# Dealing the opening order of a fused attention and SwiGLU kernel anew, with its squares summed on TensorE and constant filler products from the first instruction

## The chip, the cores and the metric

The kernel runs on one core of one Trainium2 chip. The metric is device time in microseconds (us), as the median of several runs. PE is TensorE's matmul side and PEld its weight loads, DVE is VectorE, ACT is ScalarE, POOL is GpSimd, SP is SyncE (it issues DMAs). All arithmetic is float32.

## The reference

Two stages. The first is a cross attention between 512 tokens and 32 states in each of 8 batches and 8 heads; the second is a SwiGLU feed-forward network over all 8 x (512 + 32) = 4352 rows of 512.

```python
def _attn_ref(x, state):                     # x: 8,8,512,64   state: 8,8,32,64
    scores = x @ state.T / sqrt(64)          # per batch and head
    a = softmax(scores);      xread = a @ state
    scores2 = state @ x.T / sqrt(64)
    a2 = softmax(scores2);    sread = a2 @ x
    return concatenate([xread, sread], axis=2)

def _moe_ref(x, w_gate, w_val, w_out, rms_g):   # x: 4352,512
    xn = x / sqrt(mean(x * x) + 1e-6) * rms_g
    g, val = xn @ w_gate, xn @ w_val            # 512 -> 1536
    return (silu(g) * val) @ w_out              # 1536 -> 512
```

The three weight matrices arrive as float64; `x` and `state` arrive as float32.

## The kernel before, in words

**Algebra.** A token's attention read is a product of its 256 softmax weights (8 heads x 32 states) with the states. The kernel therefore folds the states of a batch into the weights once: `own_weights(b, mp)` multiplies the states (times `rms_g`, tile `stT_g`, L390) with a block `w_m` of `w_gate` and `w_val` (L528) and copies the result to `v` (L539). The hidden layer of the batch is then `v` times the transposed softmax weights `aT_s`. The scale of the RMS norm is multiplied into `aT_s` (L434), so nothing of the hidden layer can start before that instruction.

**Tokens of a batch** (`tokens_read(b)`): transposes of `x_b` on TensorE (L298 for the first two batches) with copies (L300), scores (L307), a 32 x 32 transpose on VectorE (L316), softmax (L378 to L403), the reads (L410), their squares on ScalarE (L417, four tiles `sq`), three additions of the squares on VectorE (L420), a sum over partitions by four products with a column of ones (L424), the power -1/2 on GpSimd (L270), a spread of it by transposes (L277), and L434.

**States of a batch** (`states_read(b)`): maxima (L446), exponentials (L452), transposes (L459) and copies (L461), products with `x_b` (L471), scaling (L478), a transpose (L482) and a copy (L484). After L471 the tile `x_b` of the batch is free; there are two of them, so the loads of batch 2's `x` (16 DMAs, L122) wait for L471 of batch 0, and those of batch 3 for L471 of batch 1.

**Weights.** The float64 weights are loaded in 18 pieces of 1 MB (`load_piece`, L186), four pieces ahead. Each piece is turned to float32 by three ScalarE steps (`exponents()`, L215, L217, L220) and four VectorE steps (`values()`, L241, L244, L248, L253); the first piece goes in two halves. Six converted pairs `w_m` are stored to DRAM (`w_d`, L257) and loaded again for every batch (`fetch`, L168) into three buffers.

**Batch 0** uses plain products: hidden layer at L570, Silu at L576, gate at L580, output projection at L776. From batch 1 on both layers use a seven-product scheme (L674 hidden, L836 projection), with sums of the weights' blocks prepared on VectorE (`weight_sums`, L817) and on GpSimd (`more_of_v`, `slot_sums`, L592 to L595).

**The order.** TensorE, VectorE and ScalarE execute what `tc.manual_schedule` records, in that order. Each piece of work is a generator, and a string of letters says which generator makes its next step. `ORDER` covers batch 0 and the preparation of batch 1: `a` and `s` are tokens and states of batch 0, `A` and `S` those of batch 1, `e` and `d` the conversion, `v` the weights of batch 0, `h`, `t`, `u` its hidden layer, `p` and `c` its projection, `w` the first weights of batch 1, `k` the sums of `wo`, and `z` one filler product whose result nobody reads (`keep_awake`, L927). `PERIOD` orders each of the batches 1 to 7, and `STATES` the last stage over the 256 state rows. SP's queue follows the order in which the steps issue DMAs.

When the first `c` or `k` is met, the pools of the conversion are closed and the later ones opened:

```python
            if stream in "ck" and "s" not in seven:
                early.close()
                open_late()
                slot_sums(1)
```

Of the kernel before, what the change touches and what calls it, by code (L numbers as in the profile page):

```python
# [8 lines left out]
F32 = mybir.dt.float32  # L9
# [8 lines left out]
P = 128  # L18
# [1 line left out]
W_BUFS = 3  # L20

ORDER = (
    "aaaaaaaaddaaaaaaeaseeaasadsasszzzzzzzzzzzzzzssdsaaaasaeadesaeeazzsdasaaezzzzzzza"
    "deadaaaddeeazzzzsedaadszzzzzadaeedzzvvavdzzadeaAzzzzhdeeddtdAdAAhueheAeedtddphAe"
    "dvdvduvdphedeAedtdhApeehddeuAdddeAhdedvdtudvvpeAAAAdhdAAteAehuhpddephepdeAdAeApA"
    "dteedAAvvveAdpudAAephtdSdhAdphdeAueedhAdeAteudddeeSppAddAAdppAdAdevApvdveehhAdth"
    "AudhpdeddeedeAdteAupvdvdvphedAAtdShhutSAhpukSSSkkkwSwkpSkpwpSSckSScckkpcSwkkkwww"
    "w"
)

PERIOD = (
# [12 lines left out]
def kernel(  # L44
# [21 lines left out]
    VE, SE, GE, TE = nc.vector, nc.scalar, nc.gpsimd, nc.tensor  # L66
# [5 lines left out]
    NC = S // P  # L72
# [18 lines left out]
    seven = {}  # L91

    early = ExitStack()
# [23 lines left out]
    def load_x(b, *queues):  # L117
# [8 lines left out]
        for c in range(NC):  # L126
            (queues or (nc.sync,))[c % max(1, len(queues))].dma_start(
                out=x_sb[b][:, c].rearrange("p (h d) -> p h d", h=H),
                in_=x[b, :, P * c:P * c + P, :].rearrange("h p d -> p h d"))

    ident = consts.tile([P, P], F32, name="ident")
    make_identity(nc, ident)
    mhalf = consts.tile([P, NC], F32, name="mhalf")
    GE.memset(mhalf, -0.5)
    ones = consts.tile([P, 1], F32, name="ones")
# [131 lines left out]
    def mean_root(ss, n):  # L267

        ri = two.tile([P, NC], F32, name="ri")
        GE.tensor_tensor(out=ri[:, 0:n], in0=ss, in1=mhalf[:, 0:n], op=ALU.pow)  # L270
        return ri

    def along_rows(ri, n):

        rp = aps.tile([P, NC, P], F32, name="at")
        for c in range(n):
            TE.transpose(out=rp[:, c, :], in_=ri[:, c:c + 1].to_broadcast([P, P]), identity=ident)  # L277
        return rp.rearrange("p c t -> p (c t)")
# [88 lines left out]
    def tokens_read(b):  # L367
        packed, soft = rows.pop(b), {}
        yield from (scores if b < 2 else scores_of_blocks)(b, packed, soft)
        half = soft["half"]  # L370
        m1 = two.tile([P, 2, S // Ns], F32, name="m1")
        z1 = two.tile([P, 2, S // Ns], F32, name="z1")

        def along(t, e):
            return t[:, e].unsqueeze(2).to_broadcast([P, S // Ns, Ns])

        for e in range(2):
            VE.reduce_max(out=m1[:, e], in_=half(e), axis=AXX)  # L378
            yield
            VE.tensor_tensor(out=half(e), in0=half(e), in1=along(m1, e), op=ALU.subtract)  # L380
            yield
            SE.activation(out=half(e), in_=half(e), func=ACTF.Exp, scale=SCALE)
            yield "step"
        stT_g[b] = two.tile([P, 4, Ns], F32, name="stT_g")
        if b > 1:
            soft["st"] = aps.tile([P, 4, Ns], F32, name="at")
            TE.transpose(out=soft["st"].rearrange("p j n -> p (j n)"),
                         in_=packed.rearrange("p e d -> p (e d)"), identity=ident)
            yield
        VE.tensor_tensor(out=stT_g[b], in0=soft["st"], in1=rms_g.unsqueeze(2).to_broadcast([P, 4, Ns]),  # L390
                         op=ALU.mult)
        yield
        aT_s[b] = two.tile([P, 2, S], F32, name="aT_s")
        for e in range(2):
            VE.reduce_sum(out=z1[:, e], in_=half(e), axis=AXX)
            yield
            VE.tensor_scalar(z1[:, e], z1[:, e], 1e-9, None, op0=ALU.add)
            VE.reciprocal(z1[:, e], z1[:, e])
            yield
            VE.tensor_tensor(out=half(e), in0=half(e), in1=along(z1, e), op=ALU.mult)  # L400
            yield
            for to, blocks in soft["back"](e):
                VE.transpose(out=to, in_=blocks)  # L403
            yield "step"


        reads = [(aps, vps)[j // 2].tile([P, S], F32, name=("at", "pv")[j // 2]) for j in range(4)]
        for j in range(4):
            for e in range(2):
                TE.matmul(out=reads[j][D * e:D * e + D, :],  # L410
                          lhsT=packed[Ns * j:Ns * j + Ns, e, :],
                          rhs=aT_s[b][Ns * j:Ns * j + Ns, e],
                          start=True, stop=True)
        yield
        sq = one.tile([P, 4, S], F32, name="sq", tag="xT")
        for i, j in enumerate((2, 3, 0, 1)):
            SE.activation(out=sq[:, i, :], in_=reads[j], func=ACTF.Square, scale=DM ** -0.5)  # L417
            yield "step" if i == 3 else None
        for i, j in ((0, 1), (2, 3), (0, 2)):
            VE.tensor_tensor(out=sq[:, i, :], in0=sq[:, i, :], in1=sq[:, j, :], op=ALU.add)  # L420
            yield
        sp = aps.tile([P, NC], F32, name="at")
        for c in range(NC):
            TE.matmul(out=sp[:, c:c + 1], lhsT=sq[:, 0, P * c:P * c + P], rhs=ones,  # L424
                      start=True, stop=True)
        yield
        ss = two.tile([P, NC], F32, name="ss")
        VE.tensor_scalar(ss, sp, 1e-6, None, op0=ALU.add)
        yield "step"
        ri = mean_root(ss, NC)  # L430
        yield
        rp = along_rows(ri, NC)
        yield
        VE.tensor_tensor(out=aT_s[b], in0=aT_s[b],  # L434
                         in1=rp.unsqueeze(1).to_broadcast([P, 2, S]), op=ALU.mult)
        yield "step"
# [79 lines left out]
    def own_weights(b, mp):  # L516


        pv = []

        def products():
            w = w_sb.pop(b * (NM // 2) + mp)
            for e in range(2):
                pv.append(vps.tile([P, 4 * P], F32, name="pv") if b and mp % 2 == 0 else
                          aps.tile([P, 4 * P], F32, name="at"))
            for j in range(4):
                for e in range(2):
                    TE.matmul(out=pv[e][Ns * j:Ns * j + Ns, :],  # L528
                              lhsT=stT_g[b][D * e:D * e + D, j, :],
                              rhs=w[D * e:D * e + D, j].rearrange("p m k f -> p (m k f)"),  # L530
                              start=True, stop=True)
            fetch(b * (NM // 2) + mp + W_BUFS)
            yield

        def copies():
            v = (seven["v"] if b else v_0).tile([P, 2, 2, 2, P], F32, name="v")
            v_sb[b, mp] = v, None
            for e in range(2):
                SE.copy(v[:, e].rearrange("p m k f -> p (m k f)"), pv[e])  # L539
                yield  # L540
            if b:
                more_of_v(b, mp)
                yield

        return products(), copies()
# [42 lines left out]
    def slot_sums(b):  # L588

        tt = aT_t[b] = seven["late"].tile([P, 3, HS], F32, name="aT_t")  # L590
        b11, b12, b21, b22 = (aT_s[b][:, e, HS * i:HS * i + HS] for e in range(2) for i in range(2))
        GE.tensor_tensor(out=tt[:, 0], in0=b12, in1=b11, op=ALU.subtract)  # L592
        GE.tensor_tensor(out=tt[:, 1], in0=b22, in1=tt[:, 0], op=ALU.subtract)
        GE.tensor_tensor(out=tt[:, 2], in0=b21, in1=tt[:, 1], op=ALU.subtract)
        GE.tensor_tensor(out=b12, in0=b22, in1=b12, op=ALU.subtract)  # L595
# [304 lines left out]
    def store_tokens(b):  # L900
        def store(r, c0, n, ot):
            r0 = T * b + P * r
            nc.sync.dma_start(out=out[r0:r0 + P, c0:c0 + n], in_=ot)
        return store
# [17 lines left out]
    def keep_awake():  # L922


        ps = fz.tile([P, 2, P], F32, name="f")
        while True:
            TE.matmul(out=ps, lhsT=ident, rhs=ident.unsqueeze(1).to_broadcast([P, 2, P]),  # L927
                      start=True, stop=True)
            yield

    def first_of_batch(b):
        for mp in range(2):
            for part in own_weights(b, mp):
                yield from part
# [32 lines left out]
                            mybir.EngineType.Activation})  # L967
    with tc.manual_schedule(**by_hand):
        for stream in ORDER:
            if stream in "ck" and "s" not in seven:  # L970
                early.close()
                open_late()
                slot_sums(1)
            next(streams[stream])
    assert all(next(stream, done) is done for name, stream in streams.items() if name != "z")
    load_state(2)
# [2 lines left out]
    for b in range(1, B):  # L979
# [6 lines left out]
        p, c, k = project_seven(S, store_tokens(b))  # L986
# [6 lines left out]
        if b + 1 < B:  # L993
            streams.update(a=tokens_read(b + 1), s=states_read(b + 1),
                           w=first_products(b + 1, then))
# [9 lines left out]
    n = B * (NM // 2)  # L1005
    h, t, u = hidden_seven(NT, (state_weights, state_sums), state_tokens, True,
                           lambda mp: fetch(n + mp + W_BUFS))
    p, c, k = project_seven(NT, store_states, nc.scalar)
# [34 lines left out]
```

## Time and profile before

| | us |
|---|---|
| median of 5 runs | 791.89 (790.74 to 792.19) |
| the profiled execution | 792.19 |
| its span, first to last instruction | 790.0 |

| engine | busy us | share of the span |
|---|---|---|
| PE | 777.8 | 98% |
| PEld | 604.1 | 76% |
| DVE | 521.4 | 66% |
| ACT | 334.2 | 42% |
| POOL | 171.0 | 22% |

The share of an engine is an average over stages with different limits. From 15 to 110 us VectorE is busy for more than 9.6 of every 10 us, later for about 6.6 of every 10. The chain of waits is the list of what ended last, followed back from the last instruction; an entry gives its start, its length and the work. In a timeline an entry gives the start, the length, the engine, line, operation and operands, how many instructions were merged, and in square brackets the idle time before it and what ended it. One float32 product appears as two records on PE; a transpose appears as one.

### The profile page before, as it was taken

The page shows a single profiled execution, that of the slowest core. Times are in us where ns is not written, and L with a number is a line of the kernel's source. Part 1 is how long each engine was busy: PE and PEld are TensorE (multiplying, and loading weights), DVE is VectorE, ACT ScalarE, POOL GpSimd, SP SyncE. Part 2 cuts the span into 40 slices and gives each one's busy share as a digit, 9 for nine tenths or more (in the row PEclk, how much of TensorE's full clock was granted, in tenths as well). Part 3 has the DMA queues.
Part 4 walks back from the last instruction along what each step waited for, and adds up shares of the span by engine and source line. Part 5 has one row for each costly group of instructions (what it writes and reads, how often), then busy time and mean ns, then how long its engine had stood idle before and what let it go on. Part 6 is the DMA issues. An engine that isn't in the chain of part 4 may idle for free.

```text
span 790.0 us, 13559 instructions
## 1 busy us (share of the span) xinstructions
PE 777.8 (98%) x5478; PEld 604.1 (76%) x5478; DVE 521.4 (66%) x822; ACT 334.2 (42%) x560; POOL 171.0 (22%) x216
## 2 busy tenths in 40 slices
PE   6999999999999999999999999999999999999998
PEld 4643444788878887888878887888788887888996
DVE  4999997688338951887268833895188725781461
ACT  4998874552245323542255124532353225410320
POOL 0100003430244023420433024402341043400000
PEclk9999999999999999999999999999999999999999
DMA  9788865730075005610263007500530024201311
GB/s 286 211 288 311 275 189 168 217 122 1 24 223 197 2 17 176 218 35 17 92 215 121 1 24 216 205 2 14 197 153 12 13 93 162 107 5 36 121 54 27
DMA packets 69277, 95.77 MB, mean 121 GB/s; under 512 B 46432, under 2 KB 54112, under 8 KB 62304
## 3 DMA queue, kind: packets, MB, share of 16 engines
q1 hardware_dynamic: 67040, 94.33, 36.4%
q8 instruction: 43, 0.70, 0.4%
q10 hardware_dynamic: 2176, 0.59, 0.3%
q14 instruction: 18, 0.15, 0.1%
HBM read 79.69 MB, written 15.20 MB: 120 GB/s over the span
## 4 chain that ended last, share of the span: by engine, by line
PE 94%; DVE 5%; DMA 0%; issue 0%; ACT 0%; SPq 0%
PE f L674 37%; PE f L836 35%; PE f L776 5%; PE pv L570 4%; PE at L528 3%; PE pv L528 3%; PE at L471 1%; DVE ex L248 1%; PE at L410 1%; PE at L346 1%; PE at L459 1%; PE at L424 1%; DVE raw L244 1%; PE pv L346 1%; PE at L298 1%; DMA rows<-in_state_dram 0%
## 5 line engine op out<-in xcount | busy, mean ns | idle before, releaser
L836 PE MATMUL f<-wo,hb 128*128 128x256 f32 x540 | 123.4, 380 | 0.2 <-ACT ot L873 0.2
L674 PE MATMUL f<-aT_s,v 128*128 128x256 f32 x504 | 120.6, 382 | 0.1
L836 PEld LDWEIGHTS f<-wo,hb 128*128 128x128 f32 x540 | 101.4, 190 | 13.6 <-ACT ot L873 0.4
L674 PEld LDWEIGHTS f<-aT_s,v 128*128 128x128 f32 x504 | 94.1, 190 | 19.6 <-DVE c L736 5.0
L736 DVE TENSOR_TENSOR g<-g,f 128x512 f32<-128x512 f32 (+1 forms) x96 | 61.8, 652 | 68.5 <-PE f L674 64.0
L674 PE MATMUL f<-aT_t,vs 128*128 128x256 f32 x336 | 87.1, 381 | 0.0
L270 POOL TENSOR_TENSOR ri<-ss,mhalf 128x4 f32<-128x4 f32 x8 | 13.5, 1692 | 321.3 <-DVE s L449 210.9
L727 ACT ACTIVATE hb<-g 128x1024 f32<-128x1024 f32 (+1 forms) x48 | 48.2, 1004 | 79.2 <-DVE g L736 79.2
L836 PE MATMUL f<-wt,hs 128*128 128x256 f32 x360 | 81.0, 381 | 0.0
L836 PEld LDWEIGHTS f<-wt,hs 128*128 128x128 f32 x360 | 67.3, 190 | 14.1 <-issue 5.1
L674 PEld LDWEIGHTS f<-aT_t,vs 128*128 128x128 f32 x336 | 63.2, 190 | 15.0 <-issue 5.9
L873 ACT COPY ot<-f 128x256 f32<-128x256 f32 x60 | 21.4, 373 | 123.0 <-PE f L836 123.0
L554 POOL TENSOR_TENSOR vs<-v 128x256 f32<-128x256 f32 x42 | 31.4, 748 | 164.2 <-ACT v L539 164.1
L739 DVE SCALAR_TENSOR_TENSOR hb<-hb,g 128x1024 f32<-128x1024 f32 x42 | 53.2, 1266 | 4.6 <-ACT hb L727 4.6
L725 ACT COPY g<-f 128x512 f32<-128x512 f32 (+1 forms) x48 | 26.9, 561 | 55.8 <-PE f L674 55.8
L776 PE MATMUL f<-wo,hb 128*128 128x512 f32 x96 | 44.7, 600 | 0.0
L557 POOL TENSOR_TENSOR vs<-v,vs 128x256 f32<-128x256 f32 x42 | 44.4, 1057 | 0.0
L570 PE MATMUL pv<-aT_s,v 128*128 128x512 f32 x96 | 43.7, 594 | 0.2 <-DVE aT_s L434 0.2
L674 PE MATMUL f<-aT_t,v 128*128 128x256 f32 x168 | 43.1, 379 | 0.0
L674 PE MATMUL f<-aT_s,vs 128*128 128x256 f32 x168 | 43.1, 379 | 0.0
L836 PE MATMUL f<-wo,hs 128*128 128x256 f32 x180 | 41.1, 379 | 0.0
L836 PEld LDWEIGHTS f<-wt,hb 128*128 128x128 f32 x180 | 33.7, 190 | 9.4 <-DVE ot L881 5.0
(144 smaller groups left out, 1278.3 us busy)
## 6 DMA issues: line engine op xcount, KB each, us to landing
w_m<-w_d SPq DMA_DIRECT2D x48, 1024.0 KB, 6.3
out_dram<-ot SPq DMA_DIRECT2D x56, 128.0 KB, 1.8
raw<-in_moe_w_val_dram SPq DMA_DIRECT2D x6, 1024.0 KB, 5.6
raw<-in_moe_w_out_dram SPq DMA_DIRECT2D x6, 1024.0 KB, 8.6
x_b<-in_x_dram SPq DMA_DIRECT2D x96, 64.0 KB, 2.8
w_d<-w_m SPq DMA_DIRECT2D x6, 1024.0 KB, 4.9
raw<-in_moe_w_gate_dram SPq DMA_DIRECT2D x5, 1024.0 KB, 6.8
x_b<-in_x_dram SPq DMA_DIRECT2D x6, 256.0 KB, 5.9
```

The source lines that it names most:

```text
L528: TE.matmul(out=pv[e][Ns * j:Ns * j + Ns, :], lhsT=stT_g[b][D * e:D * e + D, j, :], rhs=w[D * e:D * e + D, j].rearrange("p m k f -> p (m k ...
L554: GE.tensor_tensor(out=vs[:, 0], in0=a21, in1=a22, op=ALU.add)
L557: GE.tensor_tensor(out=vs[:, 2], in0=a12, in1=vs[:, 1], op=ALU.subtract)
L570: TE.matmul(out=to[0], lhsT=lhs(i, k), rhs=r, start=(i == 0), stop=(i == len(rhs) - 1))
L674: TE.matmul(out=ps[:, i, 0:half], lhsT=l[:, i, :], rhs=r, start=(start and i == 0 and k == 0), stop=(k == len(lhs) - 1), skip_group_check= ...
L725: SE.copy(gates(q)[1], q["x"][:, :, 0:half])
L727: SE.activation(out=hb[:, 2 * mp:2 * mp + 2, 0:n].rearrange("p m (c t) -> p m c t", c=2), in_=q["g"][:, :, :, 0:half], func=ACTF.Silu if s ...
L736: VE.tensor_tensor(out=to, in0=to, in1=q[ps][:, :, 0:half], op=ALU.add)
L739: VE.scalar_tensor_tensor(out=h, in0=h, scalar=1.0, op0=ALU.add, op1=ALU.mult, in1=q["g"].rearrange("p m c t -> p m (c t)"))
L776: TE.matmul(out=banks[r], lhsT=hb[:, m, P * r:P * r + P], rhs=wo[:, m, :], start=(m == 0), stop=(m == NM - 1))
L836: TE.matmul(out=banks[name][:, r, :], lhsT=lhs(k)[:, P * r:P * r + P], rhs=rhs(k), start=(start and r == 0 and k == 0), stop=(k == HM - 1) ...
L873: SE.copy(to, banks[name][:, r, :])
```

## The change

Four things are edited.

1. `ORDER` is dealt anew: the same steps, with 38 fillers instead of 40. Six fillers stand at its head and 20 in a row after the scores of batch 0. The states of batch 0 (`s`), which were done between the scores and the hidden layer, stand near the end of the string, beside those of batch 1.
2. For batch 0 the three additions of squares on VectorE are left out. Instead 16 products with the column of ones, four for each of the four tiles, add up in the same PSUM columns.
3. The filler multiplies a tile `still`, filled with 1.0 by VectorE, with itself, instead of the identity that GpSimd makes.
4. `slot_sums(1)` on GpSimd becomes the first step of `w`, and `w` also closes the early pools.

```diff
@@ -20,12 +20,11 @@
 ORDER = (
-    "aaaaaaaaddaaaaaaeaseeaasadsasszzzzzzzzzzzzzzssdsaaaasaeadesaeeazzsdasaaezzzzzzza"
-    "deadaaaddeeazzzzsedaadszzzzadaeedzzvvavdzzadeaAzzzzhdeeddtdAdAAhueheAeedtddphAe"
...
-    "AudhpdeddeedeAdteAupvdvdvphedAAtdShhutSAhpukSSSkkkwSwkpSkpwpSSckSScckkpcSwkkkwww"
-    "w"
+    "zzzzzzaaaaaaaaadaedeezzaaaaaaaaaaeeaaaaaaeaeaaazzzzzzzzzzzzzzzzzzzzaeaaaeddddadd"
+    "zzzzaadddeedaaadzvdaeevddzzaeavdedzzAzhdAeAdtheeheuhAdddAdpetAeduedevvdpvepAhdAe"
...
+    "ddAdAAvAedAvAdpAsvAhSSetdhuShAdhtukkAASwsSkwkkwSpSSSSkpcpSkwskkkckSwpcSSscskwwww"
 )
@@ -128,6 +127,8 @@
+    still = early.enter_context(tc.tile_pool(name="still", bufs=1)).tile([P, 2, P], F32, name="still")
+    VE.memset(still, 1.0)
     ident = consts.tile([P, P], F32, name="ident")
@@ -416,14 +417,17 @@
-        for i, j in ((0, 1), (2, 3), (0, 2)):
+        for i, j in () if b == 0 else ((0, 1), (2, 3), (0, 2)):
             VE.tensor_tensor(out=sq[:, i, :], in0=sq[:, i, :], in1=sq[:, j, :], op=ALU.add)
             yield
         sp = aps.tile([P, NC], F32, name="at")
-        for c in range(NC):
-            TE.matmul(out=sp[:, c:c + 1], lhsT=sq[:, 0, P * c:P * c + P], rhs=ones,
-                      start=True, stop=True)
-        yield
+        n = 4 if b == 0 else 1
+        for i in range(n):
+            for c in range(NC):
+                TE.matmul(out=sp[:, c:c + 1], lhsT=sq[:, i, P * c:P * c + P], rhs=ones,
+                          start=(i == 0 and c == 0), stop=(i == n - 1), skip_group_check=True)
+            yield
@@ -924,11 +928,13 @@
         ps = fz.tile([P, 2, P], F32, name="f")
         while True:
-            TE.matmul(out=ps, lhsT=ident, rhs=ident.unsqueeze(1).to_broadcast([P, 2, P]),
+            TE.matmul(out=ps, lhsT=still[:, 0], rhs=still,
                       start=True, stop=True)
             yield
 
     def first_of_batch(b):
+        slot_sums(b)
+        yield
         for mp in range(2):
@@ -967,10 +973,9 @@
         for stream in ORDER:
-            if stream in "ck" and "s" not in seven:
+            if stream in "ckw" and "s" not in seven:
                 early.close()
                 open_late()
-                slot_sums(1)
             next(streams[stream])
```

The lines of the changed kernel stand up to five higher: L307 is L308 after the change, L316 is L317, L434 is L438, L570 is L574, L674 is L678.

On SP, 27 loads of `x` in a row (11 of batch 2, 16 of batch 3) now stand between the reloads of the fifth and the sixth `w_m` of batch 1; before, 13 stood there.

More of the change, by code (lines that the diff above doesn't have):

```diff
@@ L22 @@
 ORDER = (
-    "aaaaaaaaddaaaaaaeaseeaasadsasszzzzzzzzzzzzzzssdsaaaasaeadesaeeazzsdasaaezzzzzzza"
-    "deadaaaddeeazzzzsedaadszzzzzadaeedzzvvavdzzadeaAzzzzhdeeddtdAdAAhueheAeedtddphAe"
-    "dvdvduvdphedeAedtdhApeehddeuAdddeAhdedvdtudvvpeAAAAdhdAAteAehuhpddephepdeAdAeApA"
-    "dteedAAvvveAdpudAAephtdSdhAdphdeAueedhAdeAteudddeeSppAddAAdppAdAdevApvdveehhAdth"
-    "AudhpdeddeedeAdteAupvdvdvphedAAtdShhutSAhpukSSSkkkwSwkpSkpwpSSckSScckkpcSwkkkwww"
-    "w"
+    "zzzzzzaaaaaaaaadaedeezzaaaaaaaaaaeeaaaaaaeaeaaazzzzzzzzzzzzzzzzzzzzaeaaaeddddadd"
+    "zzzzaadddeedaaadzvdaeevddzzaeavdedzzAzhdAeAdtheeheuhAdddAdpetAeduedevvdpvepAhdAe"
+    "dtedddehAueheddApdddepvevhdddevdtdupeddeAeehAtshppAAdhduhdedddeeAveeApvdpvdstued"
+    "edAddehhtpddehetpuAddshpvdeuAsedvspAAAAApveshAhAsdtAdudedhedsehtAsAApupdeeAedApp"
+    "ddAdAAvAedAvAdpAsvAhSSetdhuShAdhtukkAASwsSkwkkwSpSSSSkpcpSkwskkkckSwpcSSscskwwww"
 )
```

## The prediction

> **What bounds the kernel now.** I read the page's chain first, because it says which engine to follow.
>
> ```profile
> span 790.0 us, 13559 instructions
> ...
> PE 777.8 (98%) x5478; PEld 604.1 (76%) x5478; DVE 521.4 (66%) x822; ACT 334.2 (42%) x560; POOL 171.0 (22%) x216
> ...
> PE 94%; DVE 5%; DMA 0%; issue 0%; ACT 0%; SPq 0%
> ```
>
> TensorE is the path for 94%. The diff touches only what runs before the period of batch 1, so I opened the chain for the first 160 us.
>
> ```profile
> 10.57 2.07 PE at L307 x16
> 12.63 0.71 DVE eS L316
> ...
> 37.34 1.14 DVE aT_s L434
> 38.52 1.98 PE pv L570 x4
> ...
> 61.43 0.14 issue
> 61.56 1.09 PE at L528 x16
> ...
> 142.11 15.74 PE f L674 x72
> 157.84 1.02 PE pv L528 x16
> 158.86 0.86 PE at L528 x16
> ```
>
> Three legs follow. To 12.6 the path is loads, transposes and the scores. From 12.6 to 38.5 it is VectorE: softmax, two weight pieces and a half, then `aT_s` (L434), the first operand of real products. From 38.5 it is TensorE, with one hole before 61.56. From 142.11 on TensorE is gapless and fed by orders the diff leaves alone, so what is won or lost by then is carried rigidly to the end.
>
> Next, the timelines of PE and DVE (start, length, instruction; two PE records make one fp32 product).
>
> ```profile
> 6.19 3.71 PE L298 MATMUL at<-ident,x_b 128*128 128x128 f32 x16
> 10.57 1.96 PE L307 MATMUL at<-xT,stT 64*32 64x512 f32 x16 [0.68 <-ACT xT L300]
> 12.46 7.41 PE L927 MATMUL f<-ident 128*128 128x256 f32 x28
> ...
> 22.58 3.29 PE L927 MATMUL f<-ident 128*128 128x256 f32 x14
> ...
> 64.50 1.09 PE L307 MATMUL at<-xT,stT 64*32 64x512 f32 x16
> ```
>
> ```profile
> 9.80 0.43 DVE L241 TENSOR_SCALAR top<-raw 128x512 int32<-128x512 int32 x1 [3.08 <-DMA raw<-in_moe_w_gate_dram]
> 10.27 0.69 DVE L244 SCALAR_TENSOR_TENSOR raw<-top,raw 128x512 f32<-128x512 int32 x1
> ...
> 30.30 1.41 DVE L420 TENSOR_TENSOR sq<-sq 128x512 f32<-128x512 f32 x2
> ```
>
> L307 takes 1.96 us at 10.57 and 1.09 at 64.50: TensorE starts at half speed. The clock column of the windows shows 1.00 there, so durations are the better witness. The filler gives the end of it: 14 records in 3.29 make 28 in about 6.5; 7.41 is 0.9 more, so about 1.8 us of it ran at half speed, to about 14.3.
>
> **The change, part by part.** The profiled execution took 792.19 us, 2.2 more than its span; the median of the runs is 791.89. I sum on this execution and apply the difference to the median.
>
> Clock. Six fillers from `still` stand ahead of the first transposes and wait only for a small memset. Half-speed fillers cost 2 x 0.44 = 0.87, so they last from about 1.0 to 6.2; rows of the state landed for L288 at 5.95, so they cost at most 0.3 there. If full speed comes by about 8, the scores run warm: the last x chunk is there at 8.1 (L298's last wait), four transposes 0.44, copy 0.59, L307 1.02, hand-overs 0.3, ready at 10.5. But VectorE first takes L241 at 9.80, which waits for a weight load, then L244 at 10.27; L316 follows at 10.27 + 0.60 = 10.87, against 12.62. **-1.75**, between 0 and that. The two fillers between L298 and L307 fit in the copy's wait when warm.
>
> VectorE to L434. Out of the stretch go the three adds of squares (0.60 + 1.32 by next starts) and the state read of batch 0, moved behind: L446 twice (0.61, 0.59), L449 0.07, L463 and L464 0.28, L478 0.30, L484 0.20. Together 3.97. What remains is less interleaved: an instruction that needs the one before it starts 0.03 after its end instead of 0.08 ahead of it. In the new order 17 such pairs stand where 9 stood, 8 x 0.12 = +0.94. **-3.03.** So L434 and the first L570 come 4.78 earlier, near 33.7.
>
> The twelve added sum products cost 0.20 each (L424: four in 0.79 by the chain), 2.4 us in all, on a TensorE that would run fillers there. VectorE covers them: it reads the sum only after the four steps of the next piece (about 4.2 us); uncovered, 2.4. On ScalarE the first half piece (0.67 + 0.73 + 0.72) now goes ahead of the two copies of scores (L318, 1.1), which end about 13; the first Exp is due at 13.3: nothing, at most 0.7 if they are late. The power on GpSimd (1.98) and L277 (0.6) lie beside four steps of the wo piece (4.2). Fillers, 38 instead of 40, cost nothing while L434 is awaited, else 0.44 each.
>
> TensorE behind 33.7. Batch 0's state read loses its free place and joins gapless work: by batch 1's pieces of the chain L459 0.44 + 0.59, L471 1.03, L482 0.11. **+2.17.** The hole before 61.56 had 0.92 idle on PE and waited for a w_m that VectorE finished late. VectorE now runs ahead in that region; I count it away, **-0.92**, between 0 and -0.92. VectorE gets 2.05 of state read back later and is full to 120, so new holes can open: at the end it has gained 1.75 + 1.92 - 0.5 = 3.2 and TensorE 4.78 - 2.17 + 0.92 = 3.5. In between TensorE is up to 1.6 ahead of its old distance, so 0 to 1.6 is the bound; I take 0, because the last piece of wo was done at 120.7 and read only from 129.
>
> Slot sums of batch 1 on GpSimd (three at 0.73 and one at 1.18) move to the first "w" step; first read at 139.10, they ended at 127.2: nothing, with 12 us of cover. Rows and fours of later batches go ahead of weight loads on SP, 0.45 each (L108: four in 1.78); the weights are loaded four pieces ahead: nothing.
>
> SP's queue. x_b of batch 0 is now freed only by its late L471, so all 16 loads of batch 2's x wait until then.
>
> ```profile
> 139.30 0.35 SPq L168 DMA_DIRECT2D w_m<-w_d x1
> 139.70 7.84 SPq L122 DMA_DIRECT2D x_b<-in_x_dram x13
> 147.64 12.51 SPq L168 DMA_DIRECT2D w_m<-w_d x4
> ```
>
> 13 x loads stood between two reloads of w_m; the second was issued at 147.64, landed 5.1 later (its issue's row) at 152.7, and is read at 158.86: 6.2 us to spare. The new order has 27 there. Seven issues went out in 3.4 us, 0.49 each, so 14 more are 6.9. The first reload goes out about 0.5 sooner against TensorE (no wait for L793 just ahead). Spare 6.2 - 6.9 + 0.5 = -0.2: a wait of 0 to 1.5, I take **+0.3**.
>
> Sum: -1.75 - 3.03 + 2.17 - 0.92 + 0.3 = -3.2 us, so 788.7.
>
> The Trainium skill, "TensorE: Matmul & The Clock Gate", Part 1, says that the gate opens after about 3.4 us of sustained activity in a free-running window; Part 4 says that transposes do not count as busy in the same way. The trace agrees: transposes from 6.19 did not open it, dense products from 10.57 did by about 14.3. By these rules, six fillers of 5.1 us fill a whole window only in some phases; otherwise the transposes behind them do not help, and the sum would be that of the first rival below.
>
> **Rivals.** First, that the fillers do not do what they are for: the clock stays half until past L307. Then L307 ends no sooner than now, 1.75 is lost, and the two fillers ahead of it add up to 1.1 (1.74 less the copy's 0.6): -1.5 to -0.4, 790.4 to 791.5. For it: half speed lasted to 14.3 although TensorE worked from 5.95. Against it: the fillers are as dense as the products that ended it.
>
> Second, slower: SP's queue. If the 27 loads issue at 0.80 each, as in the seven at 100.52 that took 5.57 behind weight traffic, they take 21.6 instead of 13.2, and the L528 that read w_m at 158.86 waits 8.4 more: +5.2 net, 797.1. It decides from 0.67 per load, where the wait reaches 4.8 and the net +1.6. Against it: no raw weights are loaded in that stretch, and the 13 loads there went at 0.49 apart from one wait.
>
> Third, holes: VectorE's inputs come late by 1.6 in the middle of the stretch and the old hole stays: -0.7 to -1.9, about 790.5.
>
> **How the numbers follow.** 0.2%, 1.6 us, is about what a measurement of this kernel can tell from no change: below 790.3 is faster, above 793.5 slower. My case has 0.72 and goes from 787.5 (0.94 sooner if the dependent pairs cost nothing, 0.3 if nothing waits for the reload) to 789.9 (1.2 later if that wait is 1.5); cold clock 0.13, nearly all within 0.2%; holes 0.08, half of it faster; slow queue 0.07. Faster 0.72 + 0.04 + 0.02 = 0.78, same 0.15, slower 0.07. The range takes in my case, half a microsecond below it for the spread of the runs (790.74 to 792.19), the holes and the better half of the cold clock: 787.0 to 791.0.
>
> **What would show it.** Right: (old line numbers) L307 about 1.1 us long, L316 starting near 10.9, L434 near 32.4, the first L570 near 33.7, no L420 in batch 0, L674's long run near 138.9, the second pair of L528 there waiting under 1 us for w_m. Wrong: L307 at 2 us; the clock falling back in the transposes; a DVE wait on ACT between 11 and 32; PE idle ahead of an L570 or L776; SP reaching the second reload less than 5.1 us ahead of its reader.

## The result and the profile after

The changed kernel takes 793.18 us (median of 21 runs, 792.06 to 795.12) against 791.80 for the kernel before (41 runs): a ratio of 1.0019, 95% interval 1.0013 to 1.0025. It is 1.4 us slower where 3.2 faster was forecast, and outside the range. Lines below are those of the changed kernel.

The page of the profiled execution: its span, the engines, and the chain's shares.

```profile
span 792.8 us, 13599 instructions
...
PE 782.5 (99%) x5498; PEld 606.5 (76%) x5498; DVE 522.9 (66%) x820; ACT 333.8 (42%) x560; POOL 171.8 (22%) x216
...
PE 94%; DVE 5%; DMA 1%; ACT 0%; issue 0%; DVEq 0%
```

Nothing shows at this height except "DMA 1%" in the chain: a transfer has joined the path. This execution took 794.63 us, 1.4 more than the median of its kernel, so something in it is dearer than usual. The chain of waits (start, length, work), front and middle:

```profile
11.03 1.30 DVE eS L317 x2
...
32.52 1.14 DVE aT_s L438
33.66 0.04 issue
33.70 1.98 PE pv L574 x4
```

```profile
134.66 0.40 DVE sr L482 x2
135.06 0.14 issue
135.19 0.41 PE at L486 x2
...
140.73 12.80 PE f L678 x59
153.54 6.34 DMA w_m<-w_d
159.87 0.04 issue
159.92 1.96 PE at L532 x16
```

The front came as computed: L317 near 11.0 (10.87), L438 at 32.5 (32.4), the first L574 at 33.70 (33.7), 4.8 ahead of before. The long run of L678 begins at 140.73 instead of 142.11: of the 4.8 only 1.4 are left, where the prediction's terms up to there leave 3.5 (4.78 less 2.17 plus 0.92). At 153.54 the chain leaves TensorE for the reload of `w_m`, and at 159.92 the profile is behind the one before. PE's timeline (start, length, instruction, idle time before it and what ended it) shows what lies between:

```profile
23.17 3.71 PE L428 MATMUL at<-ones,sq 128*128 128x1 f32 x32
...
28.34 1.96 PE L532 MATMUL at<-w_m,stT_g 64*32 64x512 f32 x16 [0.42 <-DVE ss L432]
...
124.97 0.63 PE L463 MATMUL at<-ident,e 128*128 128x128 f32 x4 [0.92 <-DVE aT_s L438]
...
135.19 0.41 PE L486 MATMUL at<-ident,sr 128*128 128x128 f32 x2 [1.06 <-DVE sr L482]
...
159.92 1.96 PE L532 MATMUL at<-w_m,stT_g 64*32 64x512 f32 x16 [2.43 <-DMA w_m<-w_d]
161.81 1.86 PE L678 MATMUL f<-aT_s,v 128*128 128x256 f32 x4
163.50 1.03 PE L678 MATMUL f<-aT_t,vs 128*128 128x256 f32 x4
```

Three things are new. There are two holes, 0.92 and 1.06, in which TensorE is idle and waits for VectorE. There is a wait of 2.43 for the sixth `w_m`. And L532 takes 1.96 twice, where a warm one takes 1.09: TensorE runs at half speed behind 28 and behind 159.9. The windows view, cut at the changes of the granted clock (stretch, length, busy time of PE, PEld, DVE, ACT, POOL, then PEclk, which is the clock granted to TensorE with 1.00 for full speed, DMA share and GB/s):

```profile
23.37:26.78 3.41, 3.41 (x33) 3.41 (x32) 3.38 (x4) 3.38 (x4) 0.00 (x0) 1.00 0.41 111
26.78:30.19 3.41, 2.99 (x19) 0.68 (x19) 3.34 (x6) 2.43 (x3) 1.39 (x1) 0.50 0.95 366
30.19:33.60 3.41, 3.11 (x23) 2.17 (x15) 3.38 (x4) 3.23 (x5) 0.00 (x0) 1.00 0.96 290
156.49:159.90 3.41, 1.00 (x16) 0.09 (x16) 3.41 (x4) 1.52 (x2) 0.26 (x1) 1.00 1.02 420
159.90:163.31 3.41, 3.39 (x20) 1.46 (x21) 1.02 (x2) 0.00 (x0) 0.00 (x0) 0.50 1.08 375
```

Each window at 0.50 is 3.41 us long and follows a window of the same length. Before the second one PE was busy for 1.00 us of 3.41, the wait. Before the first one PE was busy without a gap, but with the one-column products of L428 that the change made sixteen of (busy is meant as the profile counts it, which models the ends of products). The prediction had a half-speed window behind neither. The first one cost this execution nothing, as L574 started at 33.70 all the same. From here on three costs are to be separated: the holes, the wait, and the half-speed windows.

### The profile page after: what moved, and what is told of

It is laid out like the page before. It is cut to its first block, busy times and chain, and to the rows that moved or that the text cites. A ratio compares the mean times of both kernels' runs of the same rounds, so it can differ in the third digit from the quotient of the medians.

```text
span 792.8 us, 13599 instructions
## 1 busy us (share of the span) xinstructions
PE 782.5 (99%) x5498; PEld 606.5 (76%) x5498; DVE 522.9 (66%) x820; ACT 333.8 (42%) x560; POOL 171.8 (22%) x216
## 4 chain that ended last, share of the span: by engine, by line
PE 94%; DVE 5%; DMA 1%; ACT 0%; issue 0%; DVEq 0%
PE f L678 37%; PE f L840 35%; PE pv L574 5%; PE f L780 4%; PE at L532 3%; PE pv L532 2%; DVE wt L821 1%; PE at L411 1%; PE at L347 1%; DMA w_m<-w_d 1%; PE f L931 1%; PE at L475 1%; PE at L463 1%; PE at L428 1%; PE pv L347 1%; DVE ex L249 0%
## 5 line engine op out<-in xcount | busy, mean ns | idle before, releaser
L678 PE MATMUL f<-aT_s,v 128*128 128x256 f32 x504 | 121.6, 384 | 0.1
L678 PEld LDWEIGHTS f<-aT_s,v 128*128 128x128 f32 x504 | 94.5, 191 | 21.5 <-DVE c L740 4.2
L678 PE MATMUL f<-aT_t,vs 128*128 128x256 f32 x336 | 87.0, 381 | 0.0
L678 PEld LDWEIGHTS f<-aT_t,vs 128*128 128x128 f32 x336 | 63.3, 190 | 14.2 <-issue 5.0
L558 POOL TENSOR_TENSOR vs<-v 128x256 f32<-128x256 f32 x42 | 31.7, 756 | 164.4 <-ACT v L543 164.2
L561 POOL TENSOR_TENSOR vs<-v,vs 128x256 f32<-128x256 f32 x42 | 44.9, 1068 | 0.0
L574 PE MATMUL pv<-aT_s,v 128*128 128x512 f32 x96 | 43.7, 596 | 0.4 <-DVE aT_s L438 0.4
L678 PE MATMUL f<-aT_s,vs 128*128 128x256 f32 x168 | 43.1, 379 | 0.0
L678 PE MATMUL f<-aT_t,v 128*128 128x256 f32 x168 | 43.1, 379 | 0.0
L840 PEld LDWEIGHTS f<-wt,hb 128*128 128x128 f32 x180 | 33.7, 190 | 9.4 <-DVE ot L885 5.0
```

Source lines behind the costliest of these rows:

```text
L558: GE.tensor_tensor(out=vs[:, 0], in0=a21, in1=a22, op=ALU.add)
L561: GE.tensor_tensor(out=vs[:, 2], in0=a12, in1=vs[:, 1], op=ALU.subtract)
L574: TE.matmul(out=to[0], lhsT=lhs(i, k), rhs=r, start=(i == 0), stop=(i == len(rhs) - 1))
L678: TE.matmul(out=ps[:, i, 0:half], lhsT=l[:, i, :], rhs=r, start=(start and i == 0 and k == 0), stop=(k == len(lhs) - 1), skip_group_check= ...
L840: TE.matmul(out=banks[name][:, r, :], lhsT=lhs(k)[:, P * r:P * r + P], rhs=rhs(k), start=(start and r == 0 and k == 0), stop=(k == HM - 1) ...
```

## Experiments

All ratios are to runs of the kernel before on the same chip; the table gives them in the order of the runs.

| run | median us | ratio, 95% interval |
|---|---|---|
| changed kernel | 793.18 | 1.0019 (1.0013 to 1.0025) |
| x_later | 791.25 | 0.9991 (0.9982 to 1.0000) |
| k_behind | 795.61 | 1.0049 (1.0036 to 1.0061) |
| both | 790.39 | 0.9982 (0.9974 to 0.9991) |
| awake | 794.32 | 1.0031 (1.0019 to 1.0044) |
| squares | 794.57 | 1.0044 (1.0027 to 1.0062) |
| x_front | 792.21 | 1.0015 (1.0002 to 1.0028) |
| x_tail | 789.05 | 0.9969 (0.9957 to 0.9981) |
| x_front_tail | 789.45 | 0.9981 (0.9969 to 0.9993) |
| clock | 790.15 | 0.9980 (0.9971 to 0.9989) |
| x_tail_wide | 788.32 | 0.9956 (0.9943 to 0.9969) |
| x_tail_z3 | 788.76 | 0.9961 (0.9947 to 0.9975) |
| x_tail_adds | 791.09 | 0.9991 (0.9982 to 1.0000) |
| wide | 792.50 | 1.0013 (1.0004 to 1.0022) |
| wide_awake | 792.94 | 1.0016 (1.0007 to 1.0025) |

**The wait: x loads behind the reload (x_later).**

```diff
-            load_x(b + 2)
+            if b > 1:
+                load_x(b + 2)
...
+                if b == 1 and at == PERIOD.index("v") + 1:
+                    load_x(b + 2)
```

> The changed kernel, with the 16 loads of batch 3's x issued on SP behind the second reload of w_m instead of ahead of it; 11 loads stay ahead. Theory (SP's queue): 11 loads at 0.58 each end near 144.3 instead of 153.4, the reload lands near 150.5, seven us ahead of its reader. The wait of 2.43 us before L532 and the half-speed window behind it (L532 0.9 longer, L678 0.8 longer) both go: the span falls by 4.1, from 792.8 to 788.7, and the median from 793.2 to about 789.1. Rival (the loads only showed lateness that comes from somewhere else, such as the landing of 1 MB beside other traffic): the wait stays over 1 us, the time within 1 us of the changed kernel's.

SP's issues in the changed kernel and, in the second fence, in x_later:

```profile
137.49 0.33 SPq L169 DMA_DIRECT2D w_m<-w_d  x1
137.87 15.57 SPq L121 DMA_DIRECT2D x_b<-in_x_dram  x27
153.54 8.76 SPq L169 DMA_DIRECT2D w_m<-w_d  x4
```

```profile
138.14 0.33 SPq L169 DMA_DIRECT2D w_m<-w_d  x1
138.52 7.50 SPq L121 DMA_DIRECT2D x_b<-in_x_dram  x11
146.12 0.41 SPq L169 DMA_DIRECT2D w_m<-w_d  x1
```

The second reload goes out at 146.12 instead of 153.54, and no wait for `w_m` is left on PE, nor a half-speed window behind it. The median falls by 1.9, not by the 4.1 of the expectation. The 4.1 came from a profile that was itself 1.4 over its median, and the front of x_later's profile was 0.7 later (first L574 at 34.39 against 33.70); together these about cover the difference. That the 16 loads ahead of the reload in SP's queue make the wait is shown; by the medians they cost 1.9. Both holes, 0.92 and 1.06, are still there.

**The holes: sums of wo behind what TensorE waits for (k_behind, both).** VectorE's and GpSimd's timelines ahead of the second hole:

```profile
131.18 1.22 DVE L821 TENSOR_TENSOR wt<-wo 128x512 f32<-128x512 f32 x1
132.43 1.10 DVE L821 TENSOR_TENSOR wt<-wo,wt 128x512 f32<-128x512 f32 x1
133.46 1.21 DVE L821 TENSOR_TENSOR wo<-wo 128x512 f32<-128x512 f32 x1
134.59 0.46 DVE L482 TENSOR_SCALAR sr<-at,z 128x64 f32<-128x64 f32 x2
```

```profile
131.81 1.17 POOL L560 TENSOR_TENSOR v<-v 128x256 f32<-128x256 f32 x1
132.95 1.17 POOL L561 TENSOR_TENSOR vs<-v,vs 128x256 f32<-128x256 f32 x1
```

TensorE had L475 done at 132.2, but L482 stood in VectorE's queue behind two sums that nobody needs yet, and these take 1.1 to 1.2 us instead of 0.68 while GpSimd works. So I moved five sums back, two behind L438 and three behind L482:

```diff
-    ...AdhtukkAASwsSkwkkwSpSSSSkpcpSkwskkkckSwpcSSscskwwww
+    ...AdhtuAAkkSwsSkwkkwSpSSSSkpcpSkwskcSkkkwpcSSscskwwww
```

> The changed kernel, with two steps of the sums of wo (L821) behind the scaling of aT_s of batch 1 (L438) and three behind the second scaling of a state read (L482) instead of ahead of them. Theory (VectorE's order makes the holes): both holes of PE, 0.92 before L463 and 1.06 before L486, shrink below 0.2; the long run of L678 starts 1.8 to 2.0 earlier. First reload and x loads move with TensorE, so the wait for w_m stays between 2 and 3 us and the time falls by 1.5 to 2, to about 791.4. Rival (GpSimd's work at the same time makes VectorE late, whatever the order): the holes keep over 0.6 each. Rival on the wait: if SP does not move with TensorE, the wait grows to 4.4 and nothing is gained.

> Both edits of the two runs before it: loads of batch 3's x behind the second reload and the five sums of wo behind what TensorE waits for. Theory (the prediction failed by these two terms alone, holes 2.0 and wait with its half-speed window 4.1): the sum is 6.1 less than the changed kernel, span near 786.8, median near 787.1, that is 4.7 below the kernel before, the 3.2 of the prediction and the 0.3 of wait it had taken included, within 1.2. Rival (a later buffer or transfer takes up what is won): over 789.

Both expectations failed. The two holes went, but PE has a new one in both kernels; in k_behind:

```profile
133.48 1.10 PE L475 MATMUL at<-x_b,e2T 128*32 128x64 f32 x64 [1.91 <-DVE sr L482]
```

L475 of batch 1 now waits for the other L482, that of batch 0, which still stands behind seven sums; batch 1 can only go on when that L482 has read its PSUM tile. The hole moved because VectorE is full in this stretch: the new order among the same steps only chose who waits. k_behind is also slower than the changed kernel: its profile has two half-speed windows in front (first L574 at 35.14), a wait of 2.35 for `w_m` and a third such window behind that wait. With the loads moved as well (both), the same order is 0.9 under x_later, and over 789, as the rival had it.

**Work in the wait (awake).** Three products with a result that is overwritten, ahead of the L532 that waits:

```diff
+            if (b, mp) == (1, 5):
+                for i in range(3):
+                    TE.matmul(out=pv[0], lhsT=ident, rhs=wo[:, i, :], start=True, stop=True)
```

> The changed kernel, with three products of ident by wo rows (0.89 each, 2.66 together), whose results are overwritten, put on TensorE directly ahead of the products that wait for the sixth w_m. The wait becomes work. Theory (the idle 2.43 us make the granted clock fall for one window): no half-speed window near 160, L532 1.06 long instead of 1.96 and the first four records of L678 1.03 instead of 1.86; the span falls by 1.7 less the 0.2 that the three products are longer than the wait, about 1.5, median near 791.7. Rival (the half-speed window comes from something else, for instance from the transfers): it stays, and the time is 0 to 0.3 longer.

In the profile the theory holds: three products in 2.84, then L532 in 1.09, no window at 0.50 there, span 791.5. But the median is 794.32, 1.1 over the changed kernel, and the profiled run is the fastest of the five. That would fit a wait that is mostly shorter than in the profile that I took as typical, with no window behind it; but three of the five runs have a mean clock of 0.995 against 0.998 in the profiled one, so they may have lost time in front as well. wide and wide_awake return to this.

**The squares by themselves (squares).** The second part of the change on the kernel before, with its old order.

> The kernel before with one part of the change alone: for batch 0 the three additions of squares (L420) are left out, and sixteen one-column products instead of four sum the four tiles; the order is the old one. Theory (one-column products do not keep the clock up): behind the sixteen products, near 27 to 36, the granted clock falls to 0.5 for one or two windows of 3.41 us, as it does in every trace of the changed kernel so far and not in the kernel before. VectorE is 1.9 us shorter to L434, the cold windows cost 0 to 1.5 of that: the time falls by 0.4 to 1.9, to about 790.8. Rival (the fall of the clock in the changed kernel comes from its thinner fillers and idle gaps, not from the products): no half-speed window, the full 1.9 won.

Neither came: 794.57, 2.7 slower, and seven of the nine runs have a mean granted clock of 1.000: in these the sixteen products, which here stand between fillers, did not lower the clock. The profiled run is an outlier (800.20, half speed from 27.6 to 41.3) and does not show where the others lose. In it the first four products wait 1.74 for ScalarE's squares, and the others stand between fillers that the old order placed for another chain. This part cannot be judged apart from the new order; where the 2.7 go in the usual run stays open.

The start of this trace bears on the prediction's first term:

```profile
10.62 1.09 PE L307 MATMUL at<-xT,stT 64*32 64x512 f32 x16 [0.68 <-ACT xT L300]
```

Up to here squares runs the instructions of the kernel before, with no filler ahead and the sixteen transposes in 3.75 us (3.71 in the trace before). There L307 took 1.96; here it takes 1.09, full speed. So the clock can open behind the transposes alone: what the prediction reads from the trace and cites a page for, that transposes do not open it, holds in the trace before and not in this one, and what fillers at the head are worth differs between executions.

**Fillers between the one-column products (x_front), and VectorE's stretch thinned (x_tail), and both (x_front_tail).** x_front, on x_later, in the order after the reads:

```diff
-    zzzzaadddeedaaadzvdaee
+    zzazzadddeedzazaadzzvdaee
```

x_tail, on x_later: two sums where VectorE waited 1.5 us before the last L584, L482 of batch 0 directly behind L438, five sums at the end of the order, where VectorE had idled for 5.5 us in the run both:

```diff
-    ...AdhtukkAASwsSkwkkwSpSSSSkpcpSkwskkkckSwpcSSscskwwww
+    ...AdhtkkuAASwsSskwkwSpSSSSkpcpSwkcSkwpcSsSscwwwwkkkkk
```

> The changed kernel with the x loads of batch 3 behind the second reload (as in x_later) and with the fillers around the sixteen one-column products dealt differently: two, two, one and one filler stand between the four groups of products, two instead of one ahead of L532 (41 fillers instead of 38). Theory (a window filled with one-column products counts as idle): no half-speed window between 20 and 40, L532 near 28.3 takes 1.06 instead of 1.96, the first L574 near 33.7 in every run instead of 33.6 to 35.1; the time against x_later falls by 0.3 to 0.8 and its scatter (790.5 to 791.7) halves. Rival (the window falls because of the idle time before L532, not the products): the half-speed window stays, no gain.

> x_later with VectorE's order before 137 us changed further than in k_behind: two sums of wo (L821) where VectorE waited 1.5 us before the last L584, the second scaling of batch 0 (L482) directly behind L438, and the last five sums of wo behind both state reads, where VectorE was idle for 5.5 us. Theory (VectorE is the bound of 120 to 135, and order alone only moves the hole, as in k_behind, unless sums leave the stretch): both holes below 0.2, the long run of L678 1.8 to 2.0 earlier against x_later, 791.25 becomes about 789.3. Rival (something else holds TensorE there): a hole of over 1 us stays in another place.

> All three: x loads behind the second reload, fillers between the one-column products, VectorE's sums of wo out of the way. If the miss of the prediction is made of wait with its cold window, cold windows in front and holes, and nothing else, this kernel is the one that the prediction described: 788.7, less the 0.3 of wait, so 788.4, within 0.5. Rival (a fourth cost): over 789.5.

x_tail came as expected: PE has no hole at all between 40 and 200 us, the time is 789.05 and lies within 788.66 to 789.57. The holes were worth 2.2 (2.0 in the trace). VectorE, not TensorE, now waits at this place:

```profile
132.08 0.47 DVE L482 TENSOR_SCALAR sr<-at,z 128x64 f32<-128x64 f32 x2 [2.75 <-PE at L475]
```

GpSimd's L558 to L561, beside which VectorE now has 2.75 us free, take 0.72 to 0.73 each instead of 1.07 to 1.27.

x_front removed the half-speed window of its profile (mean granted clock 0.999), but the time did not fall: 792.21 against 791.25 for x_later. The sum is ready later (L574 at 34.27, waiting for L438), and four of its twelve runs, at a mean clock of 0.994, are 4 us longer. None of those was traced; what holds the clock down in them is open. x_front_tail inherits both: 788.62 to 789.75 us in nine runs, 792.59 to 792.86 in three, and its median of 789.45 misses the 788.4 expected.

**The first part alone (clock).** Six fillers of `still` at the head of the kernel before.

> The kernel before with the first part of the change alone: the tile still, filled by VectorE, as the filler's operand, and six fillers at the head of the order; the two fillers ahead of L307 in the changed kernel are not added, nothing else moves. Theory (the prediction's first term): L307 takes 1.09 instead of 1.96 and ends near 10.9, L316 starts near 10.9 instead of 12.63, L434 and the first L570 come 1.75 earlier, and as the rest of the order is the old one, with 13 x loads between the reloads, the time falls by 1.0 to 1.75, to about 790.3. Rival (what is won in front is lost to VectorE's inputs, weights or holes by 140): under 0.5 won.

790.15, 1.4 faster (ratio 0.9980), inside the expectation, with no later loss. VectorE's timeline:

```profile
10.38 0.69 DVE L246 SCALAR_TENSOR_TENSOR raw<-top,raw 128x512 f32<-128x512 int32 x1
10.99 1.30 DVE L318 STREAM_TRANSPOSE eS<-at 128x512 f32<-128x512 f32 x2
```

The transpose of the scores (L318 here) starts at 10.99 instead of 12.63, directly behind the L246 that the prediction had put ahead of it. In all fourteen traces with the six fillers the scores take 1.09 instead of 1.96, so the first rival is out.

**What makes the clock fall in front (x_tail_wide, x_tail_z3, x_tail_adds).** Wide: the sixteen products read the column of ones 64 times and one of 64 equal columns is used.

```diff
-        sp = aps.tile([P, NC], F32, name="at")
-        n = 4 if b == 0 else 1
+        n, wide = (4, 64) if b == 0 else (1, 1)
+        sp = aps.tile([P, NC, wide], F32, name="at")
...
+                          rhs=ones.to_broadcast([P, wide]) if b == 0 else ones,
```

z3 puts one filler behind each of the first three groups of four; adds gives the squares back to VectorE (four products, in the new order).

> x_tail with the sixteen sum products of batch 0 made 64 columns wide (the column of ones read 64 times, one of the 64 equal columns is used). Theory (a product of one column leaves the array idle for the gate although PE is busy without a gap): with 64 columns the products cost as much or up to 0.6 us more, and no half-speed window follows; L532 near 28.4 takes 1.06, the first L574 comes at 33.65 instead of 34.44, the time falls by 0.3 to 0.8 to about 788.5. Rival (the number of columns is of no matter; weight loads between short products, or gaps, close the gate): the half-speed window stays.

> x_tail with one filler behind each of the first three groups of four one-column products, nothing else changed (41 fillers). The groups then end near 28.2, when VectorE is due to read the sum. Theory: 1.33 us of fillers in the 5 us keep the window above the gate's threshold in most runs: L574 at 33.7 to 33.8, time 788.3 to 788.8. Rival (x_front's runs of clock 0.994 come from fillers between the groups): some runs 3 to 4 us longer, as there.

> x_tail with the squares of batch 0 added by VectorE as before, four one-column products instead of sixteen, in the changed kernel's order. This undoes the change's second part alone. Theory (the prediction's second term, 1.92 us of VectorE on the path to L438, less what the cold windows behind sixteen products take back): L574 near 35.4 if a cold window still follows, 35.5 with none; the time 1.0 to 1.9 over x_tail, near 790.5. Rival (cold windows cost what the squares win): within 0.5 of x_tail.

PE's timeline in x_tail and, second, in x_tail_wide:

```profile
23.12 4.29 PE L428 MATMUL at<-ones,sq 128*128 128x1 f32 x32
27.27 1.20 PE L931 MATMUL f<-still 128*128 128x256 f32 x2
28.40 1.96 PE L532 MATMUL at<-w_m,stT_g 64*32 64x512 f32 x16
...
34.44 1.98 PE L574 MATMUL pv<-aT_s,v 128*128 128x512 f32 x4
```

```profile
23.39 3.76 PE L428 MATMUL at<-ones,sq 128*128 128x64 f32 x32
26.99 0.65 PE L932 MATMUL f<-still 128*128 128x256 f32 x2
28.56 1.09 PE L533 MATMUL at<-w_m,stT_g 64*32 64x512 f32 x16 [0.92 <-DVE ss L433]
...
34.02 1.98 PE L575 MATMUL pv<-aT_s,v 128*128 128x512 f32 x4 [1.37 <-DVE aT_s L439]
```

The gap ahead of L532 is 0.92 with 64 columns. It is 0.92 too in the run both, where the products have one column, and there L532 runs at half speed:

```profile
28.28 1.96 PE L532 MATMUL at<-w_m,stT_g 64*32 64x512 f32 x16 [0.92 <-DVE ss L432]
```

And two stretches of x_tail_wide in the windows view, to be set beside the first two of the changed kernel above:

```profile
23.37:26.78 3.41, 3.41 (x32) 3.41 (x31) 3.34 (x5) 3.38 (x4) 0.00 (x0) 1.00 0.41 80
26.78:30.19 3.41, 2.49 (x25) 1.23 (x25) 3.34 (x5) 3.16 (x4) 1.39 (x1) 1.00 0.94 359
```

The same place, PE and PEld busy for the whole stretch in both, the products no dearer (3.76 against 3.71): with one column the next window runs at 0.50, with 64 at 1.00. The runs that were not traced agree: of the 27 runs of the three kernels with 64 columns, 26 have a mean clock of 0.999 or 1.000, and no run of the kernels with this front and one column has over 0.998. The number of columns is the cause; weight loads and gaps are not. The gain is 0.73, and all five runs lie within 788.20 to 788.65. z3 helps in part: four runs near 788.7, and one at 790.21, the profiled one, with two half-speed windows (L574 at 35.62). In x_tail_adds L574 comes at 36.55, and the time is 2.0 over x_tail: that is about the 1.92 of the prediction for the three additions. It is no clean measure of them, as four one-column products with idle gaps of 2.88 and 2.69 around them lose the clock as well.

**The wait again, with a quiet front (wide, wide_awake).** The changed kernel with the wide products alone, and with two products in the wait.

> The changed kernel with the sixteen sum products of batch 0 made 64 columns wide and nothing else; x loads and sums of wo stand as in the change. Theory (three separate costs that add up): no half-speed window in front, but the holes (2.0) and the wait stay: 0.7 under the changed kernel, about 792.4. In the profile the wait before L532 is 1.5 to 2.5, and a half-speed window follows it where the idle time falls into one window of 3.41 us. Rival (the fall of the clock at the wait is a sequel of that in front): no half-speed window behind the wait, 791.0.

> wide with two products of ident by wo rows (1.9 us together, overwritten) ahead of the products that wait for the sixth w_m. Theory (the idle time itself closes the gate): the wait that is left is 0.5 or less, no half-speed window follows in any run, and the time is 1.0 to 1.7 under wide if the window follows there in most runs, about 791.0. Rival (the wait is lost time, and the window behind it rare): within 0.4 of wide.

In wide, and second in wide_awake:

```profile
158.50 1.09 PE L533 MATMUL at<-w_m,stT_g 64*32 64x512 f32 x16 [1.09 <-DMA w_m<-w_d]
```

```profile
157.97 1.98 PE L533 MATMUL at<-wo,ident 128*128 128x512 f32 x4
159.88 1.09 PE L536 MATMUL at<-w_m,stT_g 64*32 64x512 f32 x16
```

wide is 0.7 under the changed kernel, as x_tail_wide was under x_tail. Its wait is 1.09, no half-speed window follows, and only one of its eleven runs has a mean clock below 0.999 (0.997, span 792.8 against 789.9 to 791.0). This profile is the fastest of the eleven, 0.5 under the median, so the usual wait may be nearer 1.6. Filling it with 1.98 of products costs 0.4, which puts it at about 1.5; both are estimates. The rival was right: the wait is lost time, 1.09 to 2.43 in the traces; the window behind it is rare, and the one in the profile of the changed kernel was not typical.

## Why the prediction was wrong

The forecast was 788.7; x_tail_wide, which keeps the change and takes out the three costs, measures 788.32, and the prediction's sum without its 0.3 of wait is 788.4. So the sum of the terms in front is borne out, also at the place where it can be read in a trace: by these terms the long run of TensorE, at 142.11 before, is due at 138.6, and in x_tail_wide it starts there. (The prediction writes 138.9, which counts a wait that comes only behind this place.)

```profile
138.57 1.13 PE L679 MATMUL f<-aT_t,vs 128*128 128x256 f32 x4
```

The miss of 4.5 is made of three steps, each measured by its removal (x_tail against x_later, x_later against the changed kernel, wide against it). Each is a difference of two medians, some from different chips, on which the kernel before took 791.55 to 792.04: it is good to about half a microsecond.

| step | in the prediction | measured |
|---|---|---|
| clock, six fillers | -1.75 | -1.4 alone, in the old order; L317 at 11.0 against 10.87 |
| VectorE to L434 | -3.03 | first L574 at 33.70 as computed |
| hole before 61.56 | -0.92 | gone |
| new holes, 120 to 136 | 0, bound 1.6 | +2.2 |
| wait for the sixth w_m | +0.3, bound 1.5 | +1.9 |
| half-speed windows behind one-column products | not in the sum | +0.7 |

2.2 + (1.9 - 0.3) + 0.7 = 4.5, from 788.7 to 793.2.

The **holes** step failed by its reason. I took 0 "because the last piece of wo was done at 120.7 and read only from 129"; but TensorE does not wait for `wo` there, it waits for `aT_s` and `sr`, which stand in VectorE's queue behind the sums of `wo`. In the trace before, the second L478 had 2.97 us of idle VectorE ahead of it:

```profile
135.24 0.47 DVE L478 TENSOR_SCALAR sr<-at,z 128x64 f32<-128x64 f32 x2 [2.97 <-PE at L471]
```

The change moved 2.05 us of state read into the stretch, and more of the sums lengthened beside GpSimd's eight steps (six took 1.09 to 1.22 up to this place, two did before): the slack was spent. The third rival named late inputs of VectorE, at 1.6 and with a chance of 0.08; the old hole, which it kept, is gone.

The **wait** step had the right mechanism and the wrong size. From the first reload to the second it is 16.05 us (137.49 to 153.54) where it was 8.34 before (139.30 to 147.64): the 14 loads more cost 7.7, not 6.9. The reader of the second came 0.4 later against the first reload, as taken (0.5). So 6.2 of spare time less 7.7 and plus 0.4 is a wait of 1.1 with a landing in 5.1, which is near what wide shows (1.09, landing in 5.2); the landing of 6.3 in the profile of the changed kernel makes it 2.4. The bound of 1.5 took no variation of the landing in. What the usual landing is stays open; the 1.9 by the medians lies between the two. One of the prediction's signs of being wrong came true: SP reached the reload at 153.54, less than 5.1 ahead of a reader that was ready at 157.49. The loads went at 0.58 each; the 0.67 from which the slower rival decides was not reached.

The **one-column products** were costed by their time on TensorE (2.4 us, covered), and that was right. What they do to the clock was not considered. Its price differs: in the traces the first L574 comes at 33.70 (changed kernel) and 33.65 (the run both), no later than with 64 columns (33.65 in wide), but also at 34.44 (x_tail) and 35.14 (k_behind); 0.7 is the difference of the medians. Nor was the first rival's question put for the middle of the kernel: it asked whether the clock opens early, not whether the new order closes it again. The Trainium skill, "TensorE: Matmul & The Clock Gate", Part 1, describes a free-running window of about 3.4 us of activity, and says that the gate falls back after one window of idleness; the windows of 3.41 us here agree. In two points the rows above differ, and they decide: a window in which PE was busy for 1.00 of 3.41 us was enough to lower the clock, and so was one that one-column products filled without a gap.

That VectorE's and GpSimd's steps lengthen each other rests on the traces alone: L821 takes 0.68 or 1.1 to 1.2, GpSimd's steps take 0.72 or 1.05 to 1.27, mostly in step with whether the other engine works. "SBUF — State Buffer" of the skill, section "SBUF: two separate sides", says that a VectorE step with two SBUF inputs and a GpSimd step that reads SBUF lock each other out of a shared port; L821 is of that kind, and the rows agree in direction. No run here kept the order and took GpSimd's work away, so its share of the 2.2 is not told apart.

x_tail_wide, the version that comes out, is faster than both kernels: 788.32, ratio 0.9956 (0.9943 to 0.9969) to the kernel before.

## What to carry to other kernels

When work is moved out of a slack place into another stretch, look there for every step that TensorE waits for and for what stands ahead of it in its engine's queue; an input that is ready early proves nothing about the queue. Where one engine is full, as VectorE was here, a new order of the same steps moved the hole, and taking work out of the stretch removed it. Compare the profiled execution's own time with the median before taking a wait in it for typical: here it was 1.4 us dear, and x_later and awake were sized by it.

## What the runs showed of the hardware

- Sixteen products of one column, PE and PEld busy for 3.41 of 3.41 us, are followed by a window of 3.41 us at a granted clock of 0.50 (changed kernel); the same products with 64 columns take as long (3.76 against 3.71 us) and are followed by 1.00 (x_tail_wide).
- The half-speed windows of the changed kernel start at 26.78 and 159.90, 39 lengths of 3.41 us apart; in x_tail the first starts at 26.08. With the same instructions in front, the first L574 came at 33.65, 33.70, 34.39, 34.44 or 35.14. The changed kernel's 21 runs span 3.1 us, the eleven of wide_awake, without half-speed windows in its trace, 0.8.
- Waits of 2.43 us (changed kernel) and 2.35 (k_behind) were followed by half speed; one of 1.09 (wide) and a hole of 1.91 (k_behind) were not.
- Sixteen transposes in 3.75 us were followed by full speed in one trace (L307 1.09, squares) and by half speed in another (L307 1.96, the kernel before).
- VectorE's two-input sums of 128x512 took 1.1 to 1.2 us beside GpSimd's and 0.68 without, and GpSimd's 128x256 steps 1.05 to 1.27 instead of 0.72.
